# An adaLN block with a KV cache: x's load and the result's store issued from the scalar engine instead of SyncE

## The chip, the cores and the metric

The kernel runs on one core of a Trainium2 chip. The metric is the device time of one execution in microseconds. One execution was also taken with the hardware profiler; its trace is what the rows below come from. The engines are named PE (TensorE, with PEld for its weight loads), DVE (VectorE), ACT (ScalarE), POOL (GpSimd) and SP (SyncE). SP computes nothing here; it only issues transfers. ACT computes and can issue transfers too. What SP issues shows as queue q1 in the trace, what ACT issues as q10.

## The reference

Two tokens (batch 2, one position) go through one transformer block with conditioning; everything is float32.

```python
mod = (silu(c) @ w_mod).reshape(2, 6, 1, 512)       # c: 2 x 512, w_mod: 512 x 3072
sa, ca, ga, sb, cb, gb = (mod[:, i] for i in range(6))
h = layernorm(x) * (1 + ca) + sa                     # x: 2 x 1 x 512
q = (h @ wq)                                         # wq: 512 x 4096, 32 heads of 128
# attention over the last 4096 positions of a cache of 32768, 8 KV heads, 4 query heads each
p = softmax(q k^T / sqrt(128));  o = p v
x = x + ga * (o @ wo)                                # wo: 4096 x 512
h = layernorm(x) * (1 + cb) + sb
x = x + gb * (silu(h @ w1) @ w2)                     # w1: 512 x 1792, w2: 1792 x 512
```

With two tokens the arithmetic is small, and the weights and the window of the cache, some 97.5 MB, are each read once. c and x are 4 KB each, and so is the result.

## The kernel before

All large operands pass through one ring in SBUF: eight slots of 16 KB in each of the 128 partitions (`RING`, L20, L68). A load takes the next one to four slots, and it can't be issued before the last reader of these slots is done. `load_runs` (L93) loads weights, `load_pair` (L82) loads two heads of K or V of one batch row. There are 26 such loads: w_mod, wq, eight of K, eight of V, two of wo, two of w1, four of w2. All are issued from SP, in the order in which they are used.

The work runs in this order:

- Start. The tile `xc` holds x and c in two halves, `x_sp` and `c_sp`, each spread over eight partition rows (`rows8` picks every 16th partition). DVE clears `xc` (L100). SP issues w_mod, then x (L109), then wq. ACT issues c in four small loads (L105).
- Constants: selection matrices from an identity, on DVE and POOL.
- Modulation. DVE transposes c (`cT`, L255 by the helper `turned`) and forms its silu with ACT (L222 to L225, L261). PE multiplies it with w_mod in two accumulators, `m_a` (L269) and `m_sp` (L272), k by k. After the first k the statistics of x (`moments`, L231 to L249) are written into the program; they use small PE matmuls for the mean (L236) and the variance (L245). DVE then forms the first layer norm's output, turned as `hq_T`.
- q. PE multiplies `hq_T` with wq (L302), and `place` puts q into the layout that the scores need (L315 to L329).
- Attention, in eight steps of two heads and one batch row: DVE turns K (L361), PE forms scores (L374), DVE and ACT form the softmax, PE multiplies with V (L448). `fetch(s + 1)` issues the next K and the present V ahead of each step.
- Output projection with wo (L579, L588), the second layer norm, the hidden layer with w1 (L627), silu, and w2 (L661, L671, L686). The last three pieces of w2 are small so that little work is left behind the last of them.
- End. DVE adds up the result in `yo` (L694 to L702), and SP issues its store (L704).

The program is written with the Tile framework, which inserts the semaphores. Where a call is wrapped in `inorder` (`tc.keep_in_program_order`) the order of the source is kept; this holds for the attention steps and most of the end. Elsewhere a list scheduler with its own estimates orders each engine's instructions: in the trace, `xT` (L508 in the source, behind the attention loop) runs at 22.24 us, directly behind the first statistics of x. The four loads of c, the load of x and the store of the result are not in `inorder`. Each transfer takes one of eight completion semaphores in turn.

Of the kernel before, what the change touches and what calls it, by code (L numbers as in the profile page):

```python
# [13 lines left out]
P = 128  # L14
# [9 lines left out]
def adaln_block(  # L24
# [19 lines left out]
    nc = tc.nc  # L44
# [43 lines left out]
    def load_runs(w, per, lo, hi):  # L88

        e = w.shape[1]  # L90
        n = -(-(hi - lo) * e // 4096)
        t = stream(n)[:, : (hi - lo) * e].rearrange("p (q e) -> p q e", e=e)
        nc.sync.dma_start(t, w.rearrange("(p q) e -> p q e", q=per)[:, lo:hi, :])  # L93
        return t


    x2 = x.rearrange("b s d -> (b s) d")
    xc = const([P, 2, P], "xc")
    x_sp, c_sp = xc[:, 0, :], xc[:, 1, :]
    nc.vector.memset(xc, 0.0)  # L100
    wm = load_runs(w_mod, 4, 0, 4)
    rows8 = lambda t: t.rearrange("(ab r) m -> ab r m", r=16)[:, 0, :]
    for b in range(B):
        for lo in (0, 2):
# [1 line left out]
                c_sp.rearrange("(g y) m -> g y m", g=4)[lo : lo + 2, 16 * b, :],  # L106
                c[b].rearrange("(g m) -> g m", m=P)[lo : lo + 2],
            )
    nc.sync.dma_start(rows8(x_sp), x2.rearrange("b (g m) -> g b m", m=P))  # L109
    wqt = load_runs(wq, 4, 0, 4)  # L110


# [151 lines left out]
    for k in range(4):  # L264
# [8 lines left out]
        if k == 0:  # L273
# [3 lines left out]
                xn, x_sp, mean_a, rstd_a, op0=ALU.subtract, op1=ALU.mult  # L277
# [299 lines left out]
    for q in range(28):  # L577
        g = q % 4
# [80 lines left out]
    for tt in range(WIDE):  # L659
        g = tt % 4  # L660
# [35 lines left out]
    yo = once.tile([P, P], F32, tag="yo", name="yo")  # L696
# [4 lines left out]
        r = slice(h * H, (h + 1) * H)  # L701
        inorder(nc.vector.tensor_add(yo[:, r], yo[:, r], yp[:, r]))  # L702
    of = out.rearrange("b s d -> (b s) d")
    nc.sync.dma_start(of.rearrange("b (g m) -> g b m", m=P), rows8(yo))  # L704


_INS = ["A_x", "A_k_cache", "A_v_cache", "A_wq", "A_wo", "B_w1", "B_w2", "c", "w_mod"]
# [24 lines left out]
```

## Time and profile before

| | us |
|---|---|
| median of 3 runs | 235.74 |
| lowest and highest run | 235.5, 236.02 |
| the profiled execution | 235.53 |
| its span in the trace | 233.7 |
| PE busy | 161.1 (69%) |
| DVE busy | 115.6 (49%) |
| ACT busy | 28.5 (12%) |
| POOL busy | 10.5 (4%) |

The span is the stretch that the trace covers, from the first instruction to the last; the execution's own time holds 1.83 us more around it. Busy time counts computing instructions; the issue of a transfer isn't counted as busy, and has a row of its own, under SPq or ACTq, whose length is the time that the issuing engine needs for it. A transfer's data move later, on 16 DMA engines that all queues share. In rows in order of time, the first number is the start in the span, the second the length, and what stands in brackets is the idle time of that engine just before, with what ended it. "x32" is a count; "128x512" is partitions by elements.

### The profile page before, as it was taken

The numbers are of one execution on the slowest core, as the hardware profiler recorded it, in microseconds if no ns is written. First come the engines' busy times: TensorE is split into PE (matmuls) and PEld (weight loads), VectorE is DVE, ScalarE is ACT, GpSimd is POOL, SyncE is SP. The second block draws the span as 40 slices with busy tenths as digits, with TensorE's granted clock in tenths as the row PEclk, the third lists the DMA queues.
The fourth block names the chain that finished last, engine by engine and source line by source line (L and its number), as shares of the span: only waits on it lengthen the run. The fifth ranks groups of instructions, "written<-read, shape, count | busy, mean of one in ns | idle before, by whom it ended". The sixth has DMA issues, their size and how long they took to land.

```text
span 233.7 us, 2571 instructions
## 1 busy us (share of the span) xinstructions
PE 161.1 (69%) x1070; PEld 43.3 (19%) x1070; DVE 115.6 (49%) x179; ACT 28.5 (12%) x64; POOL 10.5 (4%) x35
## 2 busy tenths in 40 slices
PE   0004916859577839797598749759759779789684
PEld 0001401201111111211120201202112122324222
DVE  0007240278894758695197089259559540101232
ACT  2000210000311120120210201111020120102020
POOL 2004710000000000000000000000000000000000
PEclk9999985979999977999979999988997997999999
DMA  7998998999999999999999999999999999989991
GB/s 269 446 542 359 404 494 359 446 444 421 415 421 449 446 437 415 426 426 446 449 437 409 418 437 449 449 421 412 426 444 449 443 421 437 463 367 437 424 404 57
DMA packets 3794, 97.68 MB, mean 418 GB/s; under 512 B 432, under 2 KB 456, under 8 KB 968
## 3 DMA queue, kind: packets, MB, share of 16 engines
q1 hardware_dynamic: 3768, 97.53, 97.1%
q8 instruction: 8, 0.13, 0.2%
q14 instruction: 2, 0.02, 0.0%
q10 hardware_dynamic: 16, 0.00, 0.0%
HBM read 97.53 MB, written 0.00 MB: 417 GB/s over the span
## 4 chain that ended last, share of the span: by engine, by line
DMA 60%; issue 18%; DVE 14%; PE 6%; POOL 0%; SPq 0%; POOLq 0%; ACT 0%
DMA slots<-in_A_k_cache_dram 22%; DMA slots<-in_A_wq_dram 15%; DMA slots<-in_A_v_cache_dram 12%; DMA slots<-in_B_w_dram 12%; DVE kT L361 11%; PE o L448 2%; PE q L302 2%; DVE zp L420 1%; PE acc_yw L661 1%; DVE xp L418 1%; PE qr L323 0%; PE acc_y L671 0%; DVE qT L315 0%; POOL qg L319 0%; SPq L109 0%
## 5 line engine op out<-in xcount | busy, mean ns | idle before, releaser
L361 DVE STREAM_TRANSPOSE kT<-slots 128x1024 f32<-128x1024 f32 x64 | 73.7, 1212 | 23.7 <-DMA slots<-in_A_k_cache_dram 23.6
L374 PE MATMUL s<-kT,qbd 128*32 128x512 f32 x256 | 68.6, 693 | 19.1 <-DVE kT L361 18.0
L448 PE MATMUL o<-slots,ptb 128*32 128x512 f32 x256 | 30.8, 624 | 2.1 <-DMA slots<-in_A_v_cache_dram 2.1
L374 PEld LDWEIGHTS s<-kT,qbd 128*32 128x32 f32 x256 | 9.6, 113 | 68.4 <-DVE kT L361 63.4
L269 PE MATMUL m_a<-slots,scT 128*32 128x256 f32 x32 | 4.4, 506 | 20.5 <-DVE scT L261 20.5
L302 PE MATMUL q<-slots,hq_T 128*32 128x512 f32 x64 | 8.3, 680 | 7.0 <-DMA slots<-in_A_wq_dram 7.0
L448 PEld LDWEIGHTS o<-slots,ptb 128*32 128x32 f32 x256 | 8.1, 114 | 17.9 <-issue 17.8
L404 ACT COPY bias<-bp 128x1 f32<-128x1 f32 x8 | 1.3, 159 | 77.0 <-PE bp L402 77.0
L384 DVE TENSOR_REDUCE mx<-s 128x1 f32<-128x512 f32 x8 | 5.5, 691 | 9.6 <-PE s L374 9.6
L565 PE MATMUL junk<-quad,id 128*32 128x512 f32 x22 | 10.2, 595 | 0.0
L420 DVE TENSOR_TENSOR zp<-xp,quarter 128x1024 f32<-128x1024 f32 x8 | 9.8, 1225 | 0.2
L435 ACT ACTIVATE ptb<-pT,odd 128x256 f32<-128x256 f32 x16 | 6.7, 472 | 25.6 <-PE pT L427 25.6
L255 DVE STREAM_TRANSPOSE cT<-xc 128x128 f32<-128x128 f32 x1 | 0.4, 401 | 16.7 <-DMA xc<-in_c_dram 16.7
L427 PE MATMUL pT<-zp,mix 128*32 128x256 f32 x64 | 5.7, 428 | 3.6 <-DVE zp L420 3.5
L458 ACT COPY ob<-o 128x512 f32<-128x512 f32 x8 | 4.7, 585 | 26.1 <-PE o L448 26.1
L272 PE MATMUL m_sp<-slots,scT 128*32 128x512 f32 x32 | 7.4, 738 | 0.0
L386 PE MATMUL mT<-ident,mx 128*1 128x128 f32 x16 | 3.0, 270 | 6.3 <-DVE mx L384 6.3
L315 DVE STREAM_TRANSPOSE qT<-q 128x512 f32<-128x512 f32 x2 | 1.4, 717 | 11.7 <-PE q L302 10.2
L418 DVE STREAM_TRANSPOSE xp<-pr 128x512 f32<-128x512 f32 x8 | 5.5, 686 | 3.4 <-ACT pr L406 3.4
L579 PE MATMUL acc_o<-slots,oTn 128*32 128x512 f32 x56 | 6.2, 593 | 0.7 <-DMA slots<-in_A_wo_dram 0.7
L466 PE MATMUL o_all<-ob,selh 128*64 128x128 f32 x64 | 6.0, 316 | 0.8 <-ACT ob L458 0.8
L550 DVE COPY acc_o_sb<-acc_o 128x256 f32<-128x256 f32 x1 | 0.4, 425 | 12.4 <-ACT acc_o_sb L549 12.4
(140 smaller groups left out, 93.8 us busy)
## 6 DMA issues: line engine op xcount, KB each, us to landing
slots<-in_A_k_cache_dram SPq DMA_DIRECT2D x8, 4096.0 KB, 27.4
slots<-in_A_v_cache_dram SPq DMA_DIRECT2D x8, 4096.0 KB, 27.6
slots<-in_w_mod_dram SPq DMA_DIRECT2D x1, 6144.0 KB, 17.1
slots<-in_A_wo_dram SPq DMA_DIRECT2D x1, 6144.0 KB
slots<-in_B_w_dram SPq DMA_DIRECT2D x1, 2688.0 KB
slots<-in_A_wo_dram SPq DMA_DIRECT2D x1, 2048.0 KB, 29.5
slots<-in_B_w_dram SPq DMA_DIRECT2D x1, 2048.0 KB
slots<-in_B_w_dram SPq DMA_DIRECT2D x1, 896.0 KB
```

Of the source, the lines that this page charges most:

```text
L272: nc.tensor.matmul(m_sp[r, :], scT[:, k, :], cd[:, g], start=(k == 0), stop=(k == 3))
L302: nc.tensor.matmul(q_ps[n][32 * g : 32 * g + 32, :], hq_T[:, k, :], wv[:, n, g], start=(k == 0), stop=(k == 3),)
L361: inorder(nc.vector.transpose(kT[s, j][:, 32 * c : 32 * c + 32, :], kt[s].rearrange("p (n j r) -> p j n r", j=4, r=32)[:, j, 32 * c : 32 * ...
L374: inorder(nc.tensor.matmul(s_ps[s][r : r + 32, :], qbd[h // 4][:, h % 4, b, j, :], kT[s, j][:, 32 * c : 32 * c + 32, e:32:2], start=(j == ...
L418: inorder(nc.vector.transpose(xp, pr[s]))
L420: inorder(nc.vector.tensor_mul(zp, xp[:, None, :, 0:16].to_broadcast([P, 4, 16, 16]), quarter[:, :, None, None].to_broadcast([P, 4, 16, 16 ...
L427: inorder(nc.tensor.matmul(tp[32 * i : 32 * i + 32, :], mix.rearrange("p v e -> p (v e)"), zp.rearrange("p y t x -> p (y t) x")[:, :, 4 * ...
L435: inorder(nc.scalar.activation(ptb[s % 2][:, :, e, :], tp.rearrange("p (w z) -> p w z", z=16), AF.Copy, scale=odd[:, e : e + 1],))
L448: inorder(nc.tensor.matmul(o_ps[s][r : r + 32, :], ptb[s % 2][:, w].rearrange("p e z -> p (e z)"), vt[s].rearrange("p (c w m f d) -> p c f ...
L466: inorder(nc.tensor.matmul(o_all[r : r + 64, :], selh[:, m, lo : lo + 2 * HQ], o_sb[s][:, m * DH : (m + 1) * DH], start=(s == 0 and m < 2) ...
L565: inorder(nc.tensor.matmul(junk[0:32, :], id4, quad.rearrange("p m y -> p (m y)"), start=True, stop=True,))
L579: inorder(nc.tensor.matmul(acc[32 * g : 32 * g + 32, :], oTn[:, q, :], wot[q], start=(q < 4), stop=(q >= 24),))
```

## The change

Two lines change the engine that issues a transfer. x's load is issued from ACT, in the program behind the four loads of c, and the store of the result is issued from ACT too. The 26 large loads stay on SP, and no computing instruction is added or removed.

```diff
@@ -106,7 +106,7 @@
                 c_sp.rearrange("(g y) m -> g y m", g=4)[lo : lo + 2, 16 * b, :],
                 c[b].rearrange("(g m) -> g m", m=P)[lo : lo + 2],
             )
-    nc.sync.dma_start(rows8(x_sp), x2.rearrange("b (g m) -> g b m", m=P))
+    nc.scalar.dma_start(rows8(x_sp), x2.rearrange("b (g m) -> g b m", m=P))
     wqt = load_runs(wq, 4, 0, 4)
@@ -701,7 +701,7 @@
         r = slice(h * H, (h + 1) * H)
         inorder(nc.vector.tensor_add(yo[:, r], yo[:, r], yp[:, r]))
     of = out.rearrange("b s d -> (b s) d")
-    nc.sync.dma_start(of.rearrange("b (g m) -> g b m", m=P), rows8(yo))
+    nc.scalar.dma_start(of.rearrange("b (g m) -> g b m", m=P), rows8(yo))
```

## The prediction

> **What bounds the kernel now.** I read the page's totals first, then its DMA queues, then stretches of the span, then the two ends in order of time, because the change touches one transfer at the start and one at the end.
>
> The page and the DMA view:
>
> ```profile
> span 233.7 us, 2571 instructions
> ...
> q1 hardware_dynamic: 3768, 97.53, 97.1%
> ...
> q10 hardware_dynamic: 16, 0.00, 0.0%
> ...
> slots<-in_w_mod_dram SPq DMA_DIRECT2D x1, 6144.0 KB, 17.1
> ...
> slots<-in_A_wq_dram SPq DMA_DIRECT2D x1, 35.2
> ```
>
> q1 is SP's queue and holds 97.1% of what 16 engines could spend in the span; q10 is the scalar engine's (ACT's) and holds today the four loads of c. The last two rows end with the time from issue to landing.
>
> The stretches (columns: us, busy time of PE, PEld, DVE, ACT, POOL, clock, DMA share, GB/s):
>
> ```profile
> 17.00:37.00 20.00, 9.81 (x68) 3.34 (x68) 8.09 (x31) 2.44 (x4) 7.94 (x23) 0.90 1.02 439
> 37.00:57.00 20.00, 16.07 (x94) 3.84 (x94) 10.43 (x13) 0.51 (x2) 0.47 (x2) 0.84 0.99 424
> 57.00:217.00 160.00, 123.85 (x772) 31.78 (x770) 92.50 (x116) 22.15 (x53) 0.49 (x2) 0.94 1.00 432
> 217.00:226.30 9.30, 7.38 (x44) 2.10 (x43) 2.68 (x12) 1.77 (x3) 0.00 (x0) 1.00 0.98 416
> ```
>
> From 17 us until the matmuls that end the kernel get their weights, the DMA share is 0.98 to 1.02: the stream of loads has no hole. A shift of work in the first 40 us is felt only if it opens a hole in that stream. What comes behind the stream is a serial tail (the order of time at the end, and SP's waits):
>
> ```profile
> 226.44 1.92 PE L661 MATMUL acc_yw<-slots,uT 128*32 128x512 f32 x16 [0.76 <-DMA slots<-in_B_w_dram]
> ...
> 228.47 0.37 ACT L549 COPY acc_y_sb<-acc_yw 128x256 f32<-128x256 f32 x1 [3.73 <-PE acc_yw L661]
> ...
> 230.70 0.35 DVE L702 TENSOR_TENSOR yo<-yo,yp 128x64 f32<-128x64 f32 x2
> 231.07 0.64 SPq L704 DMA_DIRECT2D out_dram<-yo  x1
> ```
> ```profile
> SPq L728 <- DMA out_dram<-yo: 0.7, 1, 0.7
> ```
>
> DVE is done at 230.70 + 0.35 = 231.05, SP issues the store from 231.07 to 231.71, and the span ends 2.0 us later (233.7). All of the store is on the path that sets the end; nothing runs beside it.
>
> **Part 1, x's load leaves SP's queue.** The start in order of time:
>
> ```profile
> 0.73 0.38 SPq L93 DMA_DIRECT2D slots<-in_w_mod_dram  x1
> ...
> 1.16 2.62 ACTq L105 DMA_DIRECT2D xc<-in_c_dram  x4
> 1.18 0.70 SPq L109 DMA_DIRECT2D xc<-in_A_x_dram  x1
> ...
> 1.93 0.58 SPq L93 DMA_DIRECT2D slots<-in_A_wq_dram  x1
> 3.82 1.28 ACT L223 ACT_TABLE_LOAD   x1 [3.82 <-issue]
> 17.88 0.40 DVE L255 STREAM_TRANSPOSE cT<-xc 128x128 f32<-128x128 f32 x1 [16.75 <-DMA xc<-in_c_dram]
> 18.31 0.23 DVE L222 TENSOR_SCALAR sgc<-cT 128x128 f32<-128x128 f32 x1
> 18.57 0.31 ACT L223 ACTIVATE sgc<-sgc 128x128 f32<-128x128 f32 x1 [13.47 <-DVE sgc L222]
> ```
>
> SP loses one issue of 0.70 us, so wq is issued at about 1.2 instead of 1.93. Worth 0: w_mod is ahead of it on the queue until 0.73 + 17.1 = 17.8, and that cover is 15.9 us. x's own 4 KB among 97.53 MB are 0.01 us of stream, and they run on the same 16 engines from either queue: 0.
>
> The Trainium skill, "DMA: Bandwidth & Descriptors", section "Issuing engines are not separate DMA queues", says that starting transfers from several engines saves the issuing engine's time and nothing else. By that saving alone the sum would be 0.70 us less if SP's issue were on the path, which the 15.9 us of cover say it isn't.
>
> **Part 2, x joins ACT's queue.** ACT issues a fifth load after c's four, and its table load at 3.82 moves back by that issue, at most 1.1 us (c's dearest, below). It would end at 6.2, and ACT next waits until 18.57: 0, with 12 us of cover.
>
> When does x land? c's 1 KB loads, all issued by 3.8, land at 17.88, as late as the 6 MB of w_mod. The 16 packets on q10 read as 4 loads of 2 rows and 2 completion counts, on two engines; that is 8 small packets an engine, and w_mod's 128 rows are 8 for each of 16. One small packet let through per large row gives just this landing. By that reading x (8 rows, on four engines by analogy 2 rows and a count each) comes after c, three turns into wq. wq lands at 1.93 + 35.2 = 37.1, so its 8 rows an engine take (37.1 - 17.8) / 8 = 2.4 us each, and x lands at 17.88 + 3 x 2.4 = 25.1. Today it is there by 22.04, when DVE reads it without waiting:
>
> ```profile
> 20.51 1.08 PE L269 MATMUL m_a<-slots,scT 128*32 128x256 f32 x8 [20.51 <-DVE scT L261]
> ...
> 22.04 0.28 DVE L231 BATCH_NORM_STATS2 st_a<-xc 128x6 f32<-128x128 f32 x1
> 22.24 0.40 DVE L255 STREAM_TRANSPOSE xT<-xc 128x128 f32<-128x128 f32 x1
> ...
> 23.23 0.59 PE L236 MATMUL mean_a<-mv_a,avg 128*128 128x1 f32 x2
> ...
> 29.08 1.84 SPq L82 DMA_DIRECT2D slots<-in_A_k_cache_dram  x2
> ...
> 30.69 0.40 DVE L255 STREAM_TRANSPOSE hq_T<-h_a 128x128 f32<-128x128 f32 x1
> ...
> 37.29 8.34 PE L302 MATMUL q<-slots,hq_T 128*32 128x512 f32 x64 [6.97 <-DMA slots<-in_A_wq_dram]
> ...
> 43.97 0.54 SPq L82 DMA_DIRECT2D slots<-in_A_v_cache_dram  x1
> ```
>
> Behind the late x on DVE stand L231, xT and the rest of the layer norm; behind that on PE the mean's matmuls and the remaining m_a and m_sp, since they are queued after L236; behind m_a the first two loads of K, which wait for w_mod's slots on SP:
>
> ```profile
> SPq L82 <- PE m_a L269: 11.7, 1, 11.7
> ```
>
> The shift is 25.1 - 22.04 = 3.1 us: K's issue at 32.2, hq_T done at 31.1 + 3.1 = 34.2. K has to be queued before wq's last row, say 2 us before 37.1 (the store above needs about 1.7 us from issue to landing, so 2 us is generous): 35.1, which leaves 2.9 us. hq_T is wanted at 37.29: 3.1 us left. V's issue at 43.97 stays, with two K loads queued ahead of it. So the delay is worth 0. If the cover were gone, every us of K's delay would be a us of the time.
>
> **Part 3, the store.** SP's row of 0.64 is replaced by an issue on ACT, whose last work ends at 228.84, so ACT waits for DVE as SP does. The trace has no 8-row transfer on ACT, and has these (least, median, greatest ns):
>
> ```profile
> L105 ACTq DMA_DIRECT2D xc<-in_c_dram x4: 485/488/1076, 1.2 to 3.3; - x4
> L109 SPq DMA_DIRECT2D xc<-in_A_x_dram x1: 701/701/701, 1.2 to 1.2; - x1
> L704 SPq DMA_DIRECT2D out_dram<-yo x1: 637/637/637, 231.1 to 231.1; - x1
> ...
> L93 SPq DMA_DIRECT2D slots<-in_w_mod_dram x1: 377/377/377, 0.7 to 0.7; - x1
> ```
>
> Lower bound: it takes what a small load of c takes, 0.49, which is 0.15 under SP's 0.64. Upper bound: ACT pays again what its first load paid over the others, 1.08 - 0.49 = 0.59. The value I take: SP issues a plain load in 0.38 where ACT needs 0.49, so ACT is 0.11 dearer and the store costs 0.64 + 0.11 = 0.75. That is nearest to the store's own row, and c's dear first issue ran beside SP's issues of x and wq, which nothing does at the end. The data's way and the closing barrier stay as they are.
>
> **Sum.** 0 + 0 + 0.11. The profiled execution took 235.53, its span 233.7 and 1.83 around it; it would become 235.64. It stands 0.21 under the median of the runs, 235.74; on the median I forecast 235.85. A measurement of this kernel tells about 0.2%, 0.47 us, from no change, so this is no change.
>
> **Rivals.** *A, ACT's issue is dear at the end (slower).* One mechanism: ACT's descriptor work is slow when it hasn't issued for long, as the 1.08 of its first load. Place: the store, with no cover. Price 0.59: 236.33. It decides from a store issue of 0.64 + 0.47 = 1.11 us. For it: the other three loads of c take 0.49, and by the end ACT hasn't issued for over 220 us. Against: c's first issue overlaps SP's 0.70, and SP's wq issue beside it is dear too (0.58 against 0.38).
>
> *B, x is so late that K's loads are (slower).* It decides from an x later than 35.1 - (29.08 - 22.04) = 28.1; then the loads stop behind wq. If Tile's order puts L231 ahead of the silu of c on DVE, m_a starts not at 20.51 but near 27.4 (x at 25.1, 0.7 of statistics and transpose, 1.6 for the rest of the silu); K's issue, 8.6 behind it, comes at 36.0, and the hole is 0.9: 236.7. If x waits for the whole of wq (37.1), K's issue comes at 37.1 + 7.0 = 44.1 and the hole is 9.0: 244.8. Against the latter: c's fourth load was issued after wq and didn't wait for it.
>
> The Trainium skill, same page, "Queues, rings and completion order", has an engine drain a packet of some 9 to 17 descriptors before it turns to another queue; by that x would land with c at 17.9 or with wq at 37.1 and not between, and c's landing at the end of w_mod fits it as well as my reading.
>
> *C, SP's issue time counts (faster).* If the first 0.70 on SP were on the path, or the store's issue on ACT were the short one besides, the time would be 235.74 - 0.70 = 235.04, or 234.9. Against: 15.9 us of cover. That the change does nothing it says isn't open: the queue is fixed by the issuing engine.
>
> **Chances and range.** Forecast (within 0.2%) 0.53; A 0.24; B with the small hole 0.05, with the large 0.02; C 0.16. Slower is A and B, 0.31; faster is C, 0.16; same 0.53. The forecast's own range is its bounds of -0.15 and +0.59 with the runs' spread of 0.26 to either side: 235.3 to 236.6. It reaches up to B's small hole, 236.7; left out are C and the large hole, 0.18 together: 235.3 to 236.7.
>
> **What would show it.** The stretch 57 to 217 us keeps its DMA share of 1.00; L231 waits for in_A_x until about 25; K's first issue moves to about 32 and stays ahead of wq's landing; the store's row on ACTq reads about 0.75. An issue over 1.1 is A; a stretch between 36 and 46 us with a DMA share well under 1 is B; a stream that ends earlier than 226.3 is C. The forecast is wrong if the store's way from issue to landing depends on the queue, which no row of before shows.

## The result, and the profile after

The changed kernel takes 237.26 us in the median (236.72 to 237.84), the kernel before on the same chip 235.68. The ratio is 1.0067, 95% interval 1.0049 to 1.0085: 1.6 us slower. The forecast was 235.85, its range 235.3 to 236.7, so the time lies outside. The profiled execution took 237.13 with a span of 235.4. One run of the experiments below, of the kernel with only DVE's order held, took 339.86 us and is left out of its ratio.

The page of the changed kernel (queues: packets, MB, share of 16 engines):

```profile
span 235.4 us, 2571 instructions
...
q1 hardware_dynamic: 3744, 97.52, 96.7%
q8 instruction: 8, 0.13, 0.2%
q10 hardware_dynamic: 40, 0.01, 0.0%
```

24 packets have moved from q1 to q10: x's and the store's. q1's share has fallen from 97.1% to 96.7% of a longer span, so somewhere SP's stream has a weak place. The start in order of time (start, length, engine, line, and in brackets the idle time before):

```profile
1.16 0.42 SPq L93 DMA_DIRECT2D slots<-in_A_wq_dram  x1
1.16 2.64 ACTq L105 DMA_DIRECT2D xc<-in_c_dram  x4
3.83 0.58 ACTq L109 DMA_DIRECT2D xc<-in_A_x_dram  x1
...
17.93 0.40 DVE L255 STREAM_TRANSPOSE cT<-xc 128x128 f32<-128x128 f32 x1 [16.80 <-DMA xc<-in_c_dram]
18.36 0.23 DVE L222 TENSOR_SCALAR sgc<-cT 128x128 f32<-128x128 f32 x1
...
24.88 0.29 DVE L231 BATCH_NORM_STATS2 st_a<-xc 128x6 f32<-128x128 f32 x1 [6.29 <-DMA xc<-in_A_x_dram]
...
25.45 0.20 DVE L224 TENSOR_SCALAR sgc<-sgc 128x128 f32<-128x128 f32 x1
...
26.67 0.29 DVE L261 TENSOR_TENSOR scT<-cT,sgc 128x128 f32<-128x128 f32 x1
...
27.73 0.58 PE L236 MATMUL mean_a<-mv_a,avg 128*128 128x1 f32 x2 [27.73 <-DVE avg L120]
29.41 0.59 PE L245 MATMUL var_a<-dm_a,avg 128*128 128x1 f32 x2 [1.09 <-DVE dm_a L241]
29.92 1.08 PE L269 MATMUL m_a<-slots,scT 128*32 128x256 f32 x8
...
36.22 1.83 SPq L82 DMA_DIRECT2D slots<-in_A_k_cache_dram  x2
...
37.84 0.40 DVE L255 STREAM_TRANSPOSE hq_T<-h_a 128x128 f32<-128x128 f32 x1
```

x lands at 24.9, as reckoned. But something else has changed that the diff doesn't show: the order on two engines. Before, DVE finished c's silu (L224, L225, L261) and then took up x (L231). Now L231 stands between L222 and L224, and the silu waits behind it for x. On PE, the mean's and the variance's matmuls now stand ahead of all of `m_a`, where the mean's stood behind its first k and the variance's behind its second. So `scT` moves from 20.16 (its reader `m_a` started at 20.51) to 26.67, `m_a` from 20.51 to 29.92, and the issue of K's first loads from 29.08 to 36.22. The same in the waits of DVE, and of SP's queue (us in total, times, longest):

```profile
DVE st_a L231 <- DMA xc<-in_A_x_dram: 6.3, 1, 6.3
```
```profile
SPq L82 <- PE m_a L269: 18.6, 1, 18.6
```

SP's wait for w_mod's slots was 11.7 and is 18.6. wq's landing is at 37.1, so K's rows are queued too late to follow it. The stretches show the weak place and show that nothing else has changed (us, busy time of PE, PEld, DVE, ACT, POOL, clock, DMA share, GB/s):

```profile
36.00:38.00 2.00, 1.44 (x20) 0.34 (x12) 1.24 (x5) 0.48 (x1) 0.00 (x0) 1.00 0.52 147
38.00:40.00 2.00, 1.71 (x16) 0.55 (x20) 1.18 (x4) 0.10 (x1) 0.73 (x2) 1.00 0.91 377
...
57.00:217.00 160.00, 124.78 (x769) 31.36 (x770) 93.00 (x111) 21.14 (x53) 0.49 (x2) 0.93 1.00 431
```

A row is counted whole in the stretch in which it begins, so a short stretch may read more or less than it holds, and shares over 1 occur; but 0.52 and 147 GB/s from 36 to 38 us is far from full. Over both stretches together, first the kernel before and then the changed one:

```profile
36.00:40.00 4.00, 2.71 (x16) 0.87 (x20) 0.00 (x0) 0.00 (x0) 0.00 (x0) 0.51 0.97 418
```
```profile
36.00:40.00 4.00, 3.15 (x36) 0.89 (x32) 2.42 (x8) 0.58 (x1) 0.73 (x2) 1.00 0.72 262
```

In these 4 us 0.62 MB fewer begin ((418 - 262) x 4), which at the 432 GB/s of the long stretch is 1.4 us, near the loss. From 57 us on the stream runs as before. The end in order of time:

```profile
228.17 1.92 PE L661 MATMUL acc_yw<-slots,uT 128*32 128x512 f32 x16 [0.75 <-DMA slots<-in_B_w_dram]
...
232.42 0.35 DVE L702 TENSOR_TENSOR yo<-yo,yp 128x64 f32<-128x64 f32 x2
232.80 0.63 ACTq L704 DMA_DIRECT2D out_dram<-yo  x1
```

The matmuls that wait for the last weights start 1.73 us later than before (228.17 against 226.44). From DVE's end (232.77) to the end of the span it is 2.6 us, as it was (231.05 to 233.7). The store, now on ACT, takes 0.63 to issue where it took 0.64.

### The profile page after: what moved, and what is told of

The parts are those of the page before. It is cut to its first block, busy times and chain, and to the rows that moved or that the text cites. A ratio compares the mean times of both kernels' runs of the same rounds, so it can differ in the third digit from the quotient of the medians.

```text
span 235.4 us, 2571 instructions
## 1 busy us (share of the span) xinstructions
PE 159.4 (68%) x1070; PEld 42.7 (18%) x1070; DVE 117.8 (50%) x179; ACT 28.5 (12%) x64; POOL 10.5 (4%) x35
## 3 DMA queue, kind: packets, MB, share of 16 engines
q1 hardware_dynamic: 3744, 97.52, 96.7%
## 4 chain that ended last, share of the span: by engine, by line
DMA 54%; issue 18%; DVE 16%; PE 9%; ACTq 1%; POOL 0%; POOLq 0%; ACT 0%; DVEq 0%
DMA slots<-in_A_k_cache_dram 22%; DMA slots<-in_A_v_cache_dram 12%; DMA slots<-in_B_w_dram 12%; DVE kT L361 11%; DMA xc<-in_A_x_dram 9%; PE o L448 2%; PE m_sp L272 2%; PE q L302 2%; PE m_a L269 1%; ACTq L105 1%; DVE zp L420 1%; PE acc_yw L661 1%; DVE xp L418 1%; DVE sgc L225 0%; PE qr L323 0%
## 5 line engine op out<-in xcount | busy, mean ns | idle before, releaser
L448 PE MATMUL o<-slots,ptb 128*32 128x512 f32 x256 | 32.1, 647 | 2.4 <-DMA slots<-in_A_v_cache_dram 2.4
L236 PE MATMUL mean_a<-mv_a,avg 128*128 128x1 f32 x2 | 0.6, 362 | 27.7 <-DVE avg L120 27.7
L427 PE MATMUL pT<-zp,mix 128*32 128x256 f32 x64 | 5.1, 386 | 4.5 <-DVE zp L420 4.5
L458 ACT COPY ob<-o 128x512 f32<-128x512 f32 x8 | 4.7, 585 | 27.4 <-PE o L448 27.4
L302 PE MATMUL q<-slots,hq_T 128*32 128x512 f32 x64 | 7.1, 594 | 0.9 <-DVE hq_T L255 0.9
L402 PE MATMUL bp<-negscale,mrow 1*128 1x1 f32 x16 | 3.0, 254 | 4.3 <-DVE mrow L395 4.3
L406 ACT ACTIVATE pr<-s,bias 128x512 f32<-128x512 f32 x8 | 5.5, 687 | 0.5 <-ACT bias L404 0.3
```

The costliest lines, as they stand in the source:

```text
L302: nc.tensor.matmul(q_ps[n][32 * g : 32 * g + 32, :], hq_T[:, k, :], wv[:, n, g], start=(k == 0), stop=(k == 3),)
L406: inorder(nc.scalar.activation(pr[s].rearrange("p t k -> p (t k)"), s_ps[s], AF.Exp, bias=bias, scale=SCALE, accum_out=rowsum[:, s : s + 1],))
L448: inorder(nc.tensor.matmul(o_ps[s][r : r + 32, :], ptb[s % 2][:, w].rearrange("p e z -> p (e z)"), vt[s].rearrange("p (c w m f d) -> p c f ...
```

## The experiments

The theory after the result: x lands late on ACT's queue; the list scheduler, which decides its order from its own estimates, puts x's statistics ahead of c's silu and so ties K's loads to x; K's first load comes too late behind wq. The rivals: the store on ACT costs something; the small loads slow the large ones; a late `hq_T`, and with it a late q, is what costs; the order itself costs.

**The two lines apart.** First, x on ACT and the store on SP:

```diff
-    nc.scalar.dma_start(of.rearrange("b (g m) -> g b m", m=P), rows8(yo))
+    nc.sync.dma_start(of.rearrange("b (g m) -> g b m", m=P), rows8(yo))
```

> Only x's load moves to ACT's queue; the store stays on SP. Theory T1 (the loss is the hole in the stream of loads behind wq: x lands at about 25, the statistics of x stand ahead of c's silu on DVE, K's first issue comes at about 36): the whole loss is here, 237.2 to 237.4, ratio to before about 1.007, K's first issue at 36. Theory T2 (the store on ACT's queue costs, by its issue or its way to memory): 235.7, ratio 1.000.

237.19 against 235.38, ratio 1.0069 (1.0052 to 1.0086). L231 starts at 24.96 and K's first load is issued at 35.98. Then the store on ACT and x on SP:

```diff
-    nc.scalar.dma_start(rows8(x_sp), x2.rearrange("b (g m) -> g b m", m=P))
+    nc.sync.dma_start(rows8(x_sp), x2.rearrange("b (g m) -> g b m", m=P))
```

> Only the store moves to ACT's queue; x stays on SP. T1: ratio 1.000 within 0.002; the issue on ACT about 0.63, the way from DVE's end to the end of the span 2.6 as before. T2: ratio about 1.007, with a longer row of the store or a longer stretch behind it.

235.37 against 235.38, ratio 0.9995 (0.9986 to 1.0004). The end of this kernel in order of time:

```profile
230.44 0.35 DVE L702 TENSOR_TENSOR yo<-yo,yp 128x64 f32<-128x64 f32 x2
230.82 0.64 ACTq L704 DMA_DIRECT2D out_dram<-yo  x1
```

The issue takes 0.64 as on SP. x's load is the whole loss; the store is free of it.

**Late x in the old order.** Both lines as changed, and the order of before held on DVE and PE:

```diff
-        nc.vector.bn_stats(st, t)
+        inorder(nc.vector.bn_stats(st, t)); inorder(nc.vector.transpose(xT, ...))
...
-        nc.vector.tensor_scalar(e, t, -1.0, 87.0, op0=ALU.mult, op1=ALU.min)
+        pin(nc.vector.tensor_scalar(e, t, -1.0, 87.0, op0=ALU.mult, op1=ALU.min))
...
-    nc.vector.tensor_mul(scT, cT, sg)
+    inorder(nc.vector.tensor_mul(scT, cT, sg))
...
-            nc.tensor.matmul(m_a[r, :], ...)
+            inorder(nc.tensor.matmul(m_a[r, :], ...))
```

`pin` is `inorder` for c's silu; the rest of the silu, `m_sp` and the mean's matmul are wrapped alike.

> Both transfers on ACT's queue as in the changed kernel, but DVE's order of before is written out (c's silu, then the constants, then the statistics of x and xT) and PE's first matmuls with w_mod stand ahead of the mean's. x still lands at about 25. T1 in the form 'the order set by Tile's scheduler turns the late x into a late K': K's first issue at 30.5 to 32.5, no hole, 235.7, ratio 1.000 within 0.002. Rival T3 (the late x alone is enough, in any order): K's first issue at 35 or later and a ratio of 1.004 or more.

235.43 against 235.38, ratio 1.0003 (0.9994 to 1.0011). Its start in order of time:

```profile
24.96 0.29 DVE L231 BATCH_NORM_STATS2 st_a<-xc 128x6 f32<-128x128 f32 x1 [2.71 <-DMA xc<-in_A_x_dram]
...
32.29 1.83 SPq L81 DMA_DIRECT2D slots<-in_A_k_cache_dram  x2
...
33.90 0.40 DVE L255 STREAM_TRANSPOSE hq_T<-h_a 128x128 f32<-128x128 f32 x1
```

x is as late as in the changed kernel (24.96 against 24.88), and nothing is lost. So neither the late x nor the small loads among the large ones cost anything: the order that the scheduler chose is needed for the loss.

**Each engine's order alone.** With only the wraps on DVE:

```diff
-        inorder(nc.tensor.matmul(sm[:, 0:1], avgm, mv[:, 0:1], ...))
+        nc.tensor.matmul(sm[:, 0:1], avgm, mv[:, 0:1], ...)
...
-            inorder(nc.tensor.matmul(m_a[r, :], ...))
+            nc.tensor.matmul(m_a[r, :], ...)
```

> Both transfers on ACT's queue; DVE's order of before is written out (c's silu, then the constants, then the statistics of x and xT), PE keeps the changed kernel's order (mean and variance ahead of w_mod's first matmuls). If DVE's order carries the loss: the mean starts at 25.7, the variance at 27.0, m_a at 27.5, K's first issue 6.3 behind that at 33.8, no hole, ratio 1.000 within 0.002. If PE's order carries it: K's issue near 36 and a ratio of 1.005 or more.

236.28 against 235.50, ratio 1.0042 (1.0024 to 1.0059), with runs spread from 235.91 to 237.59. With only the wraps on PE:

```diff
-        inorder(nc.vector.bn_stats(st, t)); ...
+        nc.vector.bn_stats(st, t)
...
-    inorder(nc.vector.tensor_mul(scT, cT, sg))
+    nc.vector.tensor_mul(scT, cT, sg)
```

> Both transfers on ACT's queue; PE's order of before for w_mod's first matmuls and the mean is written out, DVE keeps the changed kernel's order (the statistics of x inside c's silu). If DVE's order carries the loss: m_a starts at 27.0, the mean waits behind its first eight at 29.6, the variance at 31, the rest of m_a ends near 36, K's first issue at 35.5 to 36.5, ratio 1.005 to 1.008. If PE's order carries it: K's issue under 34 and ratio 1.000.

237.53 against 235.50, ratio 1.0080 (1.0067 to 1.0093). The rows of K's issue, of the first and of the second kernel:

```profile
33.16 1.83 SPq L81 DMA_DIRECT2D slots<-in_A_k_cache_dram  x2
```
```profile
34.37 1.83 SPq L81 DMA_DIRECT2D slots<-in_A_k_cache_dram  x2
```

K's issue came earlier than expected by 0.6 in the first and by more than 1.1 in the second, and yet both lost more than an issue before 35.1 should. The deadline of the prediction is wrong too. This question is taken up at the end.

**Why x lands when it does.** c in one load of eight rows, the rest as changed, and the order too:

```diff
-    for b in range(B):
-        for lo in (0, 2):
-            nc.scalar.dma_start(...)
+    nc.scalar.dma_start(rows8(c_sp), c.rearrange("b (g m) -> g b m", m=P))
```

> Both transfers on ACT's queue, the order of the changed kernel, but c comes in one load of eight rows instead of four of two, so 3 small packets an engine stand ahead of x's 3 instead of 8. If ACT's queue gets one small packet in per large row (about 1.8 us each while w_mod's 48 KB rows run): c lands at about 10, x at about 16, both before w_mod's 17.8; K's first issue at 26 to 28, no hole, 235.7, ratio 1.000 within 0.002. If x were late for another reason (its place on ACT's queue as such, or 8 rows on four engines): x at about 25 again and 237.3.

235.61 against 235.38, ratio 1.0010 (1.0001 to 1.0018).

```profile
10.49 0.40 DVE L255 STREAM_TRANSPOSE cT<-xc 128x128 f32<-128x128 f32 x1 [9.36 <-DMA xc<-in_c_dram]
...
15.92 0.29 DVE L231 BATCH_NORM_STATS2 st_a<-xc 128x6 f32<-128x128 f32 x1 [4.76 <-DMA xc<-in_A_x_dram]
...
27.67 1.83 SPq L82 DMA_DIRECT2D slots<-in_A_k_cache_dram  x2
```

With three small loads fewer on the queue x is there 9 us sooner, K's issue comes at 27.67, and the loss is nearly gone with the scheduler's new order in place. The opposite: one more load of two rows on ACT's queue, into a tile that nobody reads.

```diff
+    spare = const([P, 32], "spare").rearrange("(g y) m -> g y m", g=4)[0:2, 0, :]
+    nc.scalar.dma_start(spare, c[0].rearrange("(g m) -> g m", m=32)[0:2])
     nc.scalar.dma_start(rows8(x_sp), ...)
```

> The changed kernel with one more small load on ACT's queue ahead of c's (two rows of c into a tile that nobody reads): two more small packets on each of the two engines that carry c, so x comes two of wq's rows later, 2 x 2.4 = 4.9. By the count of packets: x's statistics start at 29.8 instead of 24.9, K's first issue at 41.1, and since the stream is already dry the time grows by the same 4.9: 242.1, ratio 1.027. If the place on ACT's queue costs a fixed delay, not one per packet: 237.3 again.

241.68 against 235.50, ratio 1.0265 (1.0246 to 1.0283).

```profile
22.50 0.40 DVE L255 STREAM_TRANSPOSE cT<-xc 128x128 f32<-128x128 f32 x1 [21.37 <-DMA xc<-in_c_dram]
29.68 0.30 DVE L231 BATCH_NORM_STATS2 st_a<-xc 128x6 f32<-128x128 f32 x1 [6.51 <-DMA xc<-in_A_x_dram]
...
41.36 1.82 SPq L80 DMA_DIRECT2D slots<-in_A_k_cache_dram  x2
```
```profile
36.00:38.00 2.00, 2.00 (x16) 0.59 (x12) 1.45 (x2) 0.47 (x2) 2.00 (x3) 1.00 0.00 0
38.00:40.00 2.00, 2.00 (x16) 0.52 (x12) 1.23 (x1) 0.00 (x0) 1.15 (x3) 1.00 0.00 0
```

A load of 256 bytes that nobody reads costs 4.6 us over the changed kernel (6.2 lost against 1.6). ACT issued it first, at 0.74, so c is later too. It moves x by 4.8 us, which is two large rows of wq (2.4 us each): one row and one count more on each of two engines, two turns later. Here the hole is plain: from 36 to 40 us no transfer begins. Last, x ahead of c on ACT's queue:

```diff
+    nc.scalar.dma_start(rows8(x_sp), ...)
     for b in range(B):
...
-    nc.scalar.dma_start(rows8(x_sp), ...)
```

> The changed kernel with x's load ahead of c's on ACT's queue. By the count of packets x lands at about 10, and now c's last load comes third into wq, at about 25: c's silu starts at 25, its product with 1.7 of constants ahead of it on DVE ends at about 29, m_a starts at 30.4, K's first issue at 36.7, 237.7, ratio 1.008 to 1.011. If only x's lateness mattered: ratio 1.000.

238.44 against 235.50, ratio 1.0114 (1.0098 to 1.0129). x is there at 10.48, and now c is last:

```profile
24.83 0.40 DVE L255 STREAM_TRANSPOSE cT<-xc 128x128 f32<-128x128 f32 x1 [13.69 <-DMA xc<-in_c_dram]
...
37.67 1.83 SPq L82 DMA_DIRECT2D slots<-in_A_k_cache_dram  x2
```

Whatever stands last on this queue comes at 24.9. K waits for c in any order, so this arrangement is the dearer one.

**How late may K's loads be?** Starting from the kernel with both orders held, matmuls into a bank that nobody reads were put on PE ahead of the last k of `m_a`, 5, 9, 14 and 19 of them:

```diff
     for k in range(4):
...
+        for j in range(5 if k == 3 else 0):
+            inorder(nc.tensor.matmul(junk0[0:32, :], scT[:, k, :], cd[:, j % 4], start=True, stop=True))
```

> The kernel with both orders held (K's loads issued at 32.29 there, ratio 1.0003) plus five matmuls of 512 columns on PE, whose result nobody reads, ahead of the last k of m_a. They take about 1.1 us, so nothing but K's issue and hq_T moves, both by that: K's issue near 33.4, hq_T near 35.4. Theory S (a smooth deadline: the loss is what K's issue is past about 34.4): no loss, ratio 0.999 to 1.001. Theory J (a jump: as soon as K's loads miss a point between 33.2 and 34.4, the stream loses some 1.1 to 1.4 us at once, and hardly more until about 36): no loss or a small one, 0.999 to 1.004, as with the order of DVE held, where K's issue was at 33.16. Theory O (it is the order on the engines and not K's issue that costs): ratio 1.000 here and in the three kernels with more matmuls.

> Nine such matmuls, about 1.9 us: K's issue near 34.2, hq_T near 36.2, still ahead of wq's landing at 37.1. Theory S: no loss, ratio 0.999 to 1.001. Theory J: K's issue is at the point where the jump lies, so 1.000 to 1.008, and if it is lost then at once by 1.1 us or more. Theory O: 1.000.

> Fourteen such matmuls, about 3.0 us: K's issue near 35.3, hq_T near 37.3. Theory S: 35.3 - 34.4 = 0.9 us lost, ratio 1.003 to 1.005. Theory J: the jump is behind it, 1.4 to 2.0 us lost, ratio 1.006 to 1.008, as with the order of PE alone held (K's issue at 34.37, ratio 1.008). Theory O: 1.000.

> Nineteen such matmuls, about 4.1 us: K's issue near 36.4, hq_T near 38.4, which is what the changed kernel has (36.22 and 37.84). Theories S and J: the changed kernel's loss, 1.6 to 2.0 us, ratio 1.007 to 1.009; then K's late issue is shown to be the whole of the loss, since x, the orders and the store are as in the kernel that lost nothing. Theory O: 1.000, or at most the 0.001 of hq_T's delay behind wq.

The ratios are 1.0006 (0.9990 to 1.0022), 1.0001 (0.9992 to 1.0011), 1.0058 (1.0037 to 1.0078) and 1.0257 (1.0235 to 1.0279). The premise of these four expectations was wrong twice: a matmul took 0.7 to 0.9 us and not 0.21 (nineteen moved `hq_T` from 33.90 to 50.30), and the first of K's two loads waits for the third k only. The row of K's issues shows it by its length, from the start of the first to the end of the second. The kernels with 9, 14 and 19 matmuls:

```profile
31.16 9.55 SPq L81 DMA_DIRECT2D slots<-in_A_k_cache_dram  x2
...
40.50 0.41 DVE L255 STREAM_TRANSPOSE hq_T<-h_a 128x128 f32<-128x128 f32 x1
```
```profile
31.87 13.84 SPq L81 DMA_DIRECT2D slots<-in_A_k_cache_dram  x2
```
```profile
32.38 18.13 SPq L81 DMA_DIRECT2D slots<-in_A_k_cache_dram  x2
```

The first load was in time in all of them. The second, an issue being 0.54, was issued at 40.2, 45.2 and 50.0. It's free at 40.2, because the first load's 4 MB last until about 37.1 + 9.7 = 46.8 (4096 KB at 432 GB/s, an estimate from the long stretch); at 45.2 it loses 1.4 us, and at 50.0 6.1 us. And `hq_T` at 40.50, 2.7 us later than in the changed kernel, costs nothing (1.0001): a late q is ruled out as the cause. What matters is K's first load. So the matmuls were put ahead of the third k instead, 2, 3, 4 and 5 of them:

```diff
-        for j in range(5 if k == 3 else 0):
+        for j in range(2 if k == 2 else 0):
```

> Both orders held, and two matmuls that nobody reads ahead of the third k (k = 2) of m_a instead of the last. The four kernels before moved only K's second load: the first waits for the third k alone. Now the first load moves too; a matmul took 0.86 us there, more while PE's clock is down, and the first load of K should be issued near 33.6 instead of 31.9 (32.29 with the orders held). Theory S (what K's first load is past 34.1 is lost, as the second load's delay cost 45.2 - 43.8 and 50.0 - 43.8): ratio 1.000, plus or minus 0.001. Theory J (a jump of 1.1 to 1.4 us somewhere between 33.2 and 34.4): 1.000 to 1.006. Theory O (K's issue doesn't matter, the orders do): 1.000 in all four.

> Three such matmuls: K's first load near 34.5. Theory S: 0.4 us lost, ratio 1.001 to 1.003. Theory J: 1.1 to 2.0 us lost, 1.005 to 1.008, as with the order of PE alone held (34.37, ratio 1.008). Theory O: 1.000.

> Four such matmuls: K's first load near 35.4. Theory S: 1.3 us lost, ratio 1.004 to 1.007. Theory J: hardly more than at 34.5, 1.006 to 1.008. Theory O: 1.000.

> Five such matmuls: K's first load near 36.2, as in the changed kernel (36.22, ratio 1.0067). Theories S and J: 1.6 to 2.1 us lost, ratio 1.006 to 1.009; then the late issue of K's first load is shown to be the whole loss. Theory O: 1.000.

K's first load came at 33.83, 35.04, 35.61 and 37.36, up to 1.2 us later than planned. All kernels in order of that issue, but for the four with matmuls ahead of the last k, where the second load came late as well (the loss is the ratio less 1, times the kernel before's 235.4 to 235.7; the last column is explained below):

| kernel | K's first issue, us | ratio (95%) | loss, us | K's first rows late by, us: mean, latest engine |
|---|---|---|---|---|
| c in one load | 27.67 | 1.0010 (1.0001 to 1.0018) | 0.2 | 0.0, 0.2 |
| the store alone on ACT | 27.90 | 0.9995 (0.9986 to 1.0004) | -0.1 | 0.0, 0.3 |
| both orders held | 32.29 | 1.0003 (0.9994 to 1.0011) | 0.1 | 0.0, 0.2 |
| DVE's order held | 33.16 | 1.0042 (1.0024 to 1.0059) | 1.0 | 0.1, 0.5 |
| both held, 2 matmuls | 33.83 | 1.0096 (1.0079 to 1.0113) | 2.3 | 0.3, 2.4 |
| PE's order held | 34.37 | 1.0080 (1.0067 to 1.0093) | 1.9 | 1.0, 3.1 |
| both held, 3 matmuls | 35.04 | 1.0069 (1.0054 to 1.0084) | 1.6 | 0.9, 1.8 |
| both held, 4 matmuls | 35.61 | 1.0088 (1.0057 to 1.0119) | 2.1 | 1.3, 1.7 |
| x alone on ACT | 35.98 | 1.0069 (1.0052 to 1.0086) | 1.6 | 1.8, 2.4 |
| the changed kernel | 36.22 | 1.0067 (1.0049 to 1.0085) | 1.6 | 1.7, 2.2 |
| both held, 5 matmuls | 37.36 | 1.0111 (1.0094 to 1.0128) | 2.6 | 3.1, 3.5 |
| x ahead of c | 37.67 | 1.0114 (1.0098 to 1.0129) | 2.7 | 3.2, 3.7 |
| one more load | 41.36 | 1.0265 (1.0246 to 1.0283) | 6.2 | 6.9, 7.3 |

In the time this is the jump (theory J), and not a smooth deadline: nothing at 32.3, 1.0 us at 33.2, about 2 us from 33.8 on, no more until 36.2, and from there 0.9 us for each us. The issue is read from one profiled execution and the ratio from several runs, which near the edge differ by 1 to 2 us, so single rows of the table are rough. Whether the issue is late because of the scheduler's order or because of idle matmuls in the old order makes no difference that these ratios tell, so the late issue is the cause, and the order acts through it.

The jump can be seen in the traces. The stretch from 36 to 38 us, with both orders held and with three matmuls added (issue at 32.29 and 35.04):

```profile
36.00:38.00 2.00, 0.73 (x8) 0.34 (x12) 0.00 (x0) 0.00 (x0) 0.00 (x0) 1.00 1.18 508
```
```profile
36.00:38.00 2.00, 1.09 (x9) 0.34 (x12) 1.92 (x6) 0.59 (x1) 0.72 (x2) 1.00 0.85 262
```

Divided by their share, the first moves 431 GB/s while busy, as the long stretch does, and the second 308 (the changed kernel 147 / 0.52 = 283). The first rows of a late K load are slow, beside any empty time. The stretches can be cut to these rows alone, first with both orders held, then in the changed kernel:

```profile
36.37:36.83 0.46, 0.00 (x0) 0.00 (x0) 0.00 (x0) 0.00 (x0) 0.00 (x0) 1.00 2.66 1140
```
```profile
36.92:37.60 0.68, 0.52 (x8) 0.00 (x0) 0.61 (x4) 0.08 (x1) 0.00 (x0) 1.00 0.00 0
37.60:38.63 1.03, 0.34 (x4) 0.16 (x8) 1.00 (x4) 0.50 (x1) 0.44 (x1) 1.00 1.59 509
```

In the first and in the third line 0.52 MB begin (1140 x 0.46 and 509 x 1.03), a row of 32 KB for each of the 16 engines. With the orders held they begin as wq's rows end and take 1.22 us each (2.66 x 0.46). In the changed kernel the first begins 1.4 us after the issue at 36.22 and the last 2.4 us after it, and they take 1.64 us each (1.59 x 1.03).

The transfer records of the traces give the start and length of every row. The table's last column is how much later K's first rows end than they would right behind wq, where a row takes 1.21 us. (The records don't name the engine; a row is put to the engine that had ended last before it.) The mean grows smoothly. It is single engines that make the jump: with the issue at 33.83, fourteen engines go from wq to K without a gap worth the name, and two begin K only between 37.3 and 38.0, up to 4.1 us after the issue. In all kernels of the table the profiled execution lost between the mean and the latest engine's delay, within 0.3 us; with the issue at 33.16, 33.83, 34.37 and 35.04 it lost 0.4, 1.4, 2.1 and 1.6. That the loads behind have to wait for the latest engine fits this, and isn't shown. Why a load that is queued 3 us ahead reaches some engines late, and why its first rows are slow, stays open.

No arrangement came out faster than the kernel before. The nearest, the store alone on ACT and both lines with the orders held, are not to be told from it.

## Why the prediction was wrong

- *Part 1, x's load leaves SP's queue, worth 0.* Right. wq was issued at 1.16 instead of 1.93 and nothing came of it; with x off SP and the orders held the ratio is 1.0003. Rival C is out.
- *Part 2, x's landing at 25.1.* Right: 24.9, by the reading of one small packet for one large row. With one load more x came at 29.68, with three fewer at 15.92, and each of these agrees. The Trainium skill, "DMA: Bandwidth & Descriptors", section "Queues, rings and completion order", has an engine take turns between the queues by whole packets, of some 9 to 17 descriptors. The turns agree with these landings. If a packet were 9 to 17 rows, x would have come with c at 17.9 or with wq at 37.1; it landed between, so a turn was one row here. How many descriptors a row of 64 KB makes, no run shows.
- *Part 2, the shift of 3.1 us.* Right for the order of before: K's issue at 32.2 and `hq_T` done at 34.2 were reckoned; with the orders held they are 32.29 and 34.30. "So the delay is worth 0" holds there, 1.0003.
- *Part 2, the step that failed.* The sum took it that L231 still stood behind c's silu on DVE. The order isn't in the diff; the list scheduler makes it anew, and it moved L231 ahead, and on PE the mean's and the variance's matmuls ahead of `m_a`. So `m_a` started at 29.92 and K's first load was issued at 36.22, where the sum had 32.2; with the old order held on both engines the loss is gone, and with it held on DVE or PE alone 1.0 and 1.9 us are lost. That it did so because its estimates have x early on ACT's queue is argued from the order alone, and no run tests it. Rival B named this very condition and had 0.05 where it was the case.
- *Rival B's sizes.* It put K's issue at 36.0, and it was 36.22, but two errors cancelled: `m_a` started at 29.92 and not near 27.4, since PE now ran the mean and the variance first, and from there to K's issue it took 6.3 us and not 8.6. Its hole of 0.9 was too small. "K has to be queued before wq's last row, say 2 us before 37.1" is the mis-sized term: the free limit lies between 32.3 and 33.2, so 3.9 to 4.8 us before, and within the next us about 2 us are lost. "Every us of K's delay would be a us of the time" holds only from an issue at 36.2 on.
- *Part 3, the store at +0.11.* Too high: 0.63 and 0.64 on ACT against 0.64 on SP, 0 in all. It was worked out from w_mod's issue against c's, and the row nearest to it, the store's own, was the better guide. Rival A is out: ACT's first issue was dear in every run (1.17 when it was x's, 1.14 when it was c in one load), but the store, some 228 us after the last issue, wasn't.

## What to carry to other kernels

A small load moved to a second queue beside a stream of large rows lands one turn later for each small packet ahead of it; count these packets, in large rows, before moving it. Where a scheduler orders instructions by its own estimates, changing an issuing engine may change the order on engines that the diff doesn't touch, so price the new wait at the earliest place where the scheduler may put its reader, and hold the order by hand if that place gates the stream. A stream has to have its next large load queued well ahead (here 3.9 to 4.8 us before the present one lands): a load that comes a little later reaches some of the engines too late, and here that cost up to some 2 us at once.

## What the runs showed of the hardware

The slow first rows and the engines that a late load reaches late were not expected; they stand above. One more: the 128x128 subtraction and scaling on DVE (L276) took 2.72 us in the changed kernel and 0.35 with the orders held. The changed kernel first:

```profile
31.22 1.83 POOL L210 MEMSET qbd<- 128x1024 f32 x2
...
31.87 2.72 DVE L276 TENSOR_SCALAR xn_a<-xc,m_a,rs_a 128x128 f32<-128x128 f32 x1
...
33.01 0.94 POOL L214 MEMSET oTn<- 128x1024 f32 x1
...
34.05 0.46 POOL L293 MEMSET uT<- 128x448 f32 x1
```
```profile
27.68 0.46 POOL L293 MEMSET uT<- 128x448 f32 x1
...
29.43 0.35 DVE L276 TENSOR_SCALAR xn_a<-xc,m_a,rs_a 128x128 f32<-128x128 f32 x1
```

The long one runs beside POOL's clearing of large tiles and ends (34.59) when the last of these ends (34.51); the short one runs after them. It's off the path here, since its reader waits for `m_a` until 36.6. That DVE waits for POOL in these rows is read from the times alone and wasn't tested.
